# A drop mask added in PSUM in place of a masked exp, and P·V in column halves, in a top-32 attention kernel

## The chip, the cores and the metric

The kernel runs on one core of a Trainium2 chip. The core has five engines that run side by side: TensorE (PE, matrix products into PSUM; its weight loads are listed apart as PEld), VectorE (DVE), ScalarE (ACT), GpSimd (POOL) and SyncE (SP, which issues DMAs). The metric is the device time of one launch in microseconds; lower is better.

## The reference

Three stages follow one another. Only the first is touched by the change.

```python
# attention: q, k, v of shape (4, 8, 576, 64)
scores = scale * np.matmul(q, k.transpose(0, 1, 3, 2))
kth = np.partition(scores, -32, axis=-1)[..., -32:-31]     # the 32nd largest of each row
scores = np.where(scores >= kth, scores, -1e9)
attn = np.exp(scores - scores.max(-1, keepdims=True))
attn = attn / (attn.sum(-1, keepdims=True) + 1e-9)
x = np.matmul(attn, v)                                     # heads joined: (2304, 512)
# routing: each token to one of 8 experts, 288 tokens each; then the expert's relu FFN
# last: h = x @ w_in;  out = (h * cos(h)) @ w_out
```

So of each row of 576 scores only those not below the 32nd largest keep their exp, and the rest must weigh nothing in the product with V.

## The kernel before

**Tiles and groups.** The attention is cut into 144 tiles of 128 queries by 576 keys: for each of 16 pairs of heads four tiles of the one head, four of the other, and a ninth tile in which each head has its last 64 queries. Four tiles make a group, 36 groups in all.

**A step.** `run` (L429) goes through 42 steps. In one step seven groups are worked on, each at another stage, and four rounds u = 0 to 3 take one tile of each group:

- group A (newest): scores, two products of 288 keys into the PSUM tile `sp` (`qk_mm`, L185), copied by ACT to `S` (`qk_ev`, L189);
- group B: the eight largest of each of eight chunks of 72 keys on DVE (`chunks`, L195), and from them a lower bound of the threshold (`thresh`);
- group C: ACT forms a sign against that bound with its row sum (L226) and the exp `E` (L228); POOL multiplies sign and scores to `W` (`below`, L232);
- group D: DVE takes the eight largest of `W` (L244) and picks the exact 32nd score by rank (L241, `oh`; the table of ranks `R8` lies in the PSUM tile `av`); then `probs` (L253 to L269) makes the masked exp `P`. `PATTERN = "adap"` says how, by the tile's place in the group: `a`, a Sign on ACT (L266) and a product on POOL (L269); `d`, one instruction on DVE that compares and multiplies (L262); `p`, a comparison (L268) and a product (L269), both on POOL. The last eight tiles are `d`;
- group E: PE transposes `P` in blocks of 128 keys by a product with the identity (`tr` L277, `tr_tail` L283, 4.5 blocks for each tile), and ACT takes them out of PSUM with a Relu (L287, L293);
- group F: PE multiplies the turned P with V (`av`, L308 and L309), five products for each tile of 65 columns (64 of V and a column of ones for the sum). For a full tile all 128 queries are one product; the ninth tile of a pair has five products for the 64 queries of the one head, then five for the other;
- group G: DVE divides by the sum (`fin`, L315 to L338).

An fp32 product stands in the trace as two passes, each a weight load and a matmul; a transpose is one. Where a pair of heads is finished, its part of the routing logits is added: four transposes and a copy in one step (`logits_t`), five small products in the next (`logits_m`, L385).

**What sets the order.** Each engine's queue is the program's order, written out in `run`: the order of the calls within a round is the order on every engine, and semaphores tie the engines together. PSUM has eight banks: `sp` takes two twice, `pt` one twice, `av` and `ptail` one each.

The slow attention (`run_slow`) is for inputs that a check at the end flags, and does not run here.

## Time and profile before

| | us |
|---|---|
| median of three runs | 1247.97 |
| lowest, highest | 1246.42, 1253.18 |
| the profiled execution | 1246.51 |
| its span, first to last instruction | 1244.7 |
| steps in their steady state (scores of group 5 to group 36) | 43.4 to 429.7 |
| busy in the whole span: PE, DVE, ACT, POOL | 1131.7, 1058.9, 787.8, 603.3 |

The span is the sum of stages with different limits, so shares of the whole span say little. Attention fills roughly the first 480 us; what follows it is mostly PE. In the views below a step is seen best between two instructions that come once in each step, and idle time by what ended it. A matmul's duration in the trace runs past the start of the next one, since matmuls are pipelined: what a matmul costs is read from the distance between starts.

### The profile page before, as it was taken

The numbers are of one execution on the slowest core, as the hardware profiler recorded it, in microseconds if no ns is written. First come the engines' busy times: TensorE is split into PE (matmuls) and PEld (weight loads), VectorE is DVE, ScalarE is ACT, GpSimd is POOL, SyncE is SP. The second block draws the span as 40 slices with busy tenths as digits, with TensorE's granted clock in tenths as the row PEclk, the third lists the DMA queues.
The fourth block names the chain that finished last, engine by engine and source line by source line (L and its number), as shares of the span: only waits on it lengthen the run. The fifth ranks groups of instructions, "written<-read, shape, count | busy, mean of one in ns | idle before, by whom it ended". The sixth has DMA issues, their size and how long they took to land.

```text
span 1244.7 us, 22829 instructions
## 1 busy us (share of the span) xinstructions
PE 1131.7 (91%) x7449; PEld 996.6 (80%) x7449; DVE 1058.9 (85%) x4172; ACT 787.8 (63%) x1539; POOL 603.3 (48%) x592
## 2 busy tenths in 40 slices
PE   6799999999999986688898989989889999999996
PEld 4588787787878776578888889978777998999985
DVE  7999999999999984687888878699999668777774
ACT  6999989989998951333445446655655545444442
POOL 5999989989998960211000020164665343121120
PEclk9999999989998986698999989999898999999998
DMA  5111121121111001455555567522321100000000
GB/s 124 38 45 38 38 70 32 32 70 32 32 32 39 2 1 39 155 171 164 189 175 167 172 197 240 178 68 85 130 93 67 35 26 18 26 26 27 26 26 29
DMA packets 61890, 98.07 MB, mean 79 GB/s; under 512 B 30912, under 2 KB 30912, under 8 KB 61248
## 3 DMA queue, kind: packets, MB, share of 16 engines
q1 hardware_dynamic: 53648, 74.47, 19.6%
q10 hardware_dynamic: 5136, 12.60, 3.0%
q0 software_dynamic: 2976, 9.44, 2.3%
q8 instruction: 61, 1.00, 0.3%
q14 instruction: 69, 0.57, 0.1%
HBM read 78.66 MB, written 17.83 MB: 78 GB/s over the span
## 4 chain that ended last, share of the span: by engine, by line
PE 36%; DVE 32%; ACT 13%; issue 9%; POOL 5%; DMA 4%; POOLq 0%; DVEq 0%; SPq 0%; ACTq 0%
PE pa L1326 10%; PE y L1374 10%; DVE C L195 5%; PE pa L1174 4%; PE y L1189 4%; ACT sg L226 4%; DMA row<-x,i 3%; DVE w L244 3%; ACT E L228 3%; ACT S L189 2%; DVE wu L1256 2%; PE sp L185 2%; ACT PT L287 2%; PE av L308 2%; DVE ct L1334 2%
## 5 line engine op out<-in xcount | busy, mean ns | idle before, releaser
L1326 PE MATMUL pa<-yh,wu 128*128 128x384 f32 x1152 | 222.3, 340 | 10.7 <-POOL yh L1310 4.8
L1374 PE MATMUL y<-wu,gh 128*128 128x512 f32 x864 | 222.7, 402 | 5.6 <-POOL gh L1362 4.9
L1326 PEld LDWEIGHTS pa<-yh,wu 128*128 128x128 f32 x1152 | 206.0, 189 | 22.4 <-POOL yh L1310 6.4
L232 POOL TENSOR_TENSOR W<-sg,S 128x576 f32<-128x576 bf16 x144 | 197.8, 1379 | 33.0 <-ACT sg L226 31.6
L1374 PEld LDWEIGHTS y<-wu,gh 128*128 128x128 f32 x864 | 164.2, 192 | 38.9 <-POOL gh L1362 6.5
L185 PE MATMUL sp<-kT,qz 128*128 128x288 f32 x512 | 175.7, 433 | 12.7 <-ACT S L189 7.4
L195 DVE MAX8 C<-S 128x8 f32<-128x72 f32 x1152 | 162.5, 215 | 6.5 <-ACT S L189 6.3
L308 PE MATMUL av<-vm,PT 128*128 128x65 f32 (+1 forms) x1216 | 150.5, 274 | 13.7 <-DVE xb L331 7.5
L308 PEld LDWEIGHTS av<-vm,PT 128*128 128x128 f32 (+1 forms) x1216 | 139.1, 190 | 20.4 <-DVE xb L331 11.4
L1358 ACT ACTIVATE gh<-cx 128x384 fp32r<-128x384 f32 x95 | 49.9, 525 | 143.4 <-DVE cx L1356 140.9
L1151 POOL DMA_INDIRECT row<-x,i x24 | 29.5, 1231 | 215.9 <-DVE hh L1181 34.4
L269 POOL TENSOR_TENSOR P<-sg,E 128x576 f32<-128x576 bf16 x102 | 131.4, 1288 | 3.8
L1174 PE MATMUL pa<-xh,wu 128*128 128x288 f32 x768 | 124.9, 314 | 0.0
L277 PEld LDWEIGHTS pt<-ident,P 128*128 128x128 f32 x576 | 80.2, 145 | 52.7 <-POOL P L269 11.5
L1189 PE MATMUL y<-hh,wu 128*128 128x288 f32 x768 | 120.1, 306 | 0.0
L277 PE MATMUL pt<-ident,P 128*128 128x128 f32 x576 | 110.7, 279 | 6.0 <-POOL P L269 4.6
L1174 PEld LDWEIGHTS pa<-xh,wu 128*128 128x128 f32 x768 | 112.1, 201 | 3.2 <-issue 2.9
L226 ACT ACTIVATE sg<-S,tb 128x576 bf16<-128x576 f32 x144 | 111.7, 775 | 1.2
L228 ACT ACTIVATE E<-S,nmx 128x576 f32<-128x576 f32 x144 | 110.8, 769 | 0.0
L1189 PEld LDWEIGHTS y<-hh,wu 128*128 128x128 f32 x768 | 109.2, 196 | 1.7 <-ACT hh L1180 0.8
L189 ACT ACTIVATE S<-sp 128x576 f32<-128x576 f32 x144 | 92.5, 642 | 27.8 <-PE sp L185 27.7
L244 DVE MAX8 w<-W 128x8 f32<-128x576 f32 x144 | 104.6, 746 | 1.3 <-POOL W L232 1.2
(243 smaller groups left out, 2149.8 us busy)
## 6 DMA issues: line engine op xcount, KB each, us to landing
raw<-in_moe_w_dram SPq DMA_DIRECT2D x63, 512.0 KB, 3.9
kT<-in_k_dram SPq DMA_DIRECT2D x16, 288.0 KB, 3.2
qz<-in_q_dram SPq DMA_DIRECT2D x32, 128.0 KB, 3.2
vm<-in_v_dram SPq DMA_DIRECT2D x32, 128.0 KB, 3.0
x<-xb SPq DMA_DIRECT2D x4, 1024.0 KB, 4.1
r<-in_moe_w_in_dram ACTq DMA_DIRECT2D x8, 512.0 KB, 4.9
r<-in_moe_w_out_dram ACTq DMA_DIRECT2D x8, 512.0 KB, 5.0
half<-in_moe_w_in_dram SPq DMA_DIRECT2D x8, 512.0 KB, 3.7
```

The costliest lines, as they stand in the source:

```text
L185: s.nc.tensor.matmul(s.SP[j][:, c, :288], lh, s.KT[p][:, o + c * 288:o + c * 288 + 288], start=True, stop=True)
L195: s.nc.vector.max(c[:, e, :], s.SS[j][:, 72 * e:72 * e + 72])
L226: A.activation(s.SG[j], s.SS[j], AF.Sign, bias=s.TB[g][:, u:u + 1], scale=-EPS1, accum_out=s.SUM[g][:, u:u + 1])
L228: A.activation(s.EX[j], s.SS[j], AF.Exp, bias=s.NMX[g][:, u:u + 1])
L232: s.nc.gpsimd.tensor_tensor(s.W[j], s.SG.pop(j), s.SS[j], op=OP.mult)
L244: V.max(w8[:, u, :], s.W.pop(4 * g + u))
L277: s.nc.tensor.transpose(s.PT[j][:, i * 128:(i + 1) * 128], s.PB[j // 2][:, o + i * 128:o + (i + 1) * 128], s.k.ident)
L308: PEe.matmul(o[lo:hi, u, :], s.PT[j][:, c * 128 + lo:c * 128 + hi], t[:, a, c, :], start=c == 0, stop=False)
L1174: PEe.matmul(p, w[:, a, f * 128:(f + 1) * 128], XH[e, c][:, b, :], start=n == 0, stop=n == 11)
L1189: PEe.matmul(Y[e][m], w[:, a, o + m * 128:o + (m + 1) * 128], t[:, b, :], start=f == 0 and i == 0, stop=f == 7 and i == 2)
L1326: s.nc.tensor.matmul(p, w[:, a, f * 128:(f + 1) * 128], s.YH[q, c][:, b, :], start=n == 0, stop=n == 11)
L1374: PEe.matmul(O[q][m], g[:, a, m * 128:(m + 1) * 128], w[:, b, c:c + 512], start=first and j == 0, stop=last and j == 2)
```

## The change

Five edits, all in the attention:

1. The exp goes straight into `P`, unmasked; `E` is gone.
2. `probs` becomes `drops`: it writes no product, only a bf16 tile `mk` that is zero where the score stays and positive where it is dropped. Pattern "papp": `p`, POOL compares (is_lt); `a`, ACT takes a Relu of 2^64 times (threshold minus score); `d`, DVE compares, for the last eight tiles alone.
3. `turn` replaces each transpose by two products into the same block of PSUM: the transpose of `P`, and on top of it the product of `mk` with -4 times the identity, `minus`, in bf16. What is dropped becomes negative there, and the Relu that takes the block out of PSUM makes it zero.
4. `av` makes every product in two halves of 64 queries, in turn: chunk 0 for the first half, chunk 0 for the second, chunk 1 for the first, and so on.
5. The rank table `R8` moves from the bank of `av` to that of `ptail`, and both are now placed differently: `ptail` is one fixed bank, `av` a tile of the pool with one buffer.

```diff
--- before.py
+++ after.py
@@ -21,6 +21,7 @@
 
 EPS1 = 1.0 - 2.0 ** -24
 BIG = 2e37
+STEEP = 2.0 ** 64
 NB = 64
 NS, NR = 24, 4
 MAGIC = 1.5 * 2.0 ** 23
@@ -113,16 +114,18 @@
 class Attention:
 
 
-    PATTERN = "adap"
+    PATTERN = "papp"
 
     def __init__(s, k, sb, ps, slow=False):
         s.k, s.nc, s.sb, s.ps, s.slow = k, k.nc, sb, ps, slow
         s.tiles = head_tiles()
-        s.nsp, s.ntail = (1, 2) if slow else (2, 1)
+        s.nsp = 1 if slow else 2
         G = s.nc.gpsimd
-
-        s.B2 = ps.tile([128, 512], F32, name="av")
-        s.R8 = s.B2[:, 260:268]
+        s.minus = sb.tile([128, 128], BF, name="minus")
+        s.nc.vector.tensor_scalar(s.minus, k.ident, -4.0, None, op0=OP.mult)
+
+        s.B1 = ps.tile([128, 512], F32, name="ptail")
+        s.R8 = s.B1[:, 256:264]
         s.nc.vector.tensor_copy(s.R8, k.rank8)
 
         s.XB, s.XT = {0: s.x_tile()}, {0: s.x_tile(0)}
@@ -145,7 +148,7 @@
             s.QZ.append(z)
         s.QT, s.KT, s.SP, s.SS, s.CC, s.TB, s.NMX, s.SUM, s.M3 = ({} for _ in range(9))
         s.todo, s.turned = [], []
-        s.SG, s.EX, s.W, s.TB2, s.PB, s.PT, s.PTL, s.PTS, s.AVP = ({} for _ in range(9))
+        s.SG, s.MK, s.W, s.TB2, s.PB, s.PT, s.PTL, s.PTS, s.AVP = ({} for _ in range(9))
 
     def x_tile(s, tail=None):
         if tail is None:
@@ -224,8 +227,9 @@
             A.activation(s.TB[g], s.M3.pop(g)[:, :, 7], AF.Copy, scale=EPS1)
         s.SG[j] = sb.tile([128, S], BF, name="sg", bufs=5)
         A.activation(s.SG[j], s.SS[j], AF.Sign, bias=s.TB[g][:, u:u + 1], scale=-EPS1, accum_out=s.SUM[g][:, u:u + 1])
-        s.EX[j] = sb.tile([128, S], F32, name="E", bufs=10)
-        A.activation(s.EX[j], s.SS[j], AF.Exp, bias=s.NMX[g][:, u:u + 1])
+        if j % 2 == 0:
+            s.PB[j // 2] = sb.tile([128, 2 * S], F32, name="P", bufs=8)
+        A.activation(s.PB[j // 2][:, S * (j % 2):S * (j % 2) + S], s.SS[j], AF.Exp, bias=s.NMX[g][:, u:u + 1])
 
     def below(s, j):
         s.W[j] = s.sb.tile([128, S], F32, name="W", bufs=6)
@@ -248,39 +252,42 @@
         pick(3)
         yield
         s.TB2[g] = sb.tile([128, 4], F32, name="tb2", bufs=2)
-        s.nc.gpsimd.tensor_scalar(s.TB2[g], T, -EPS1, None, op0=OP.mult)
-
-    def probs(s, j, kind):
+        s.nc.gpsimd.tensor_scalar(s.TB2[g], T, STEEP, None, op0=OP.mult)
+
+    def drops(s, j, kind):
 
         nc, sb = s.nc, s.sb
         g, u = divmod(j, 4)
         T = s.k.tall[:, 1, j:j + 1]
-        if j // 2 not in s.PB:
-            s.PB[j // 2] = sb.tile([128, 2 * S], F32, name="P", bufs=5)
-        P = s.PB[j // 2][:, S * (j % 2):S * (j % 2) + S]
-        if kind == "d":
-            nc.vector.scalar_tensor_tensor(P, s.SS[j], T, s.EX[j], op0=OP.is_ge, op1=OP.mult)
-            return
-        m = sb.tile([128, S], BF, name="sg2", bufs=4)
+        if j // 2 not in s.MK:
+            s.MK[j // 2] = sb.tile([128, 2 * S], BF, name="mk", bufs=5)
+        m = s.MK[j // 2][:, S * (j % 2):S * (j % 2) + S]
         if kind == "a":
-            nc.scalar.activation(m, s.SS[j], AF.Sign, bias=s.TB2[g][:, u:u + 1], scale=EPS1)
+
+            nc.scalar.activation(m, s.SS[j], AF.Relu, bias=s.TB2[g][:, u:u + 1], scale=-STEEP)
         else:
-            (nc.vector if kind == "m" else nc.gpsimd).tensor_scalar(m, s.SS[j], T, None, op0=OP.is_ge)
-        nc.gpsimd.tensor_tensor(P, m, s.EX[j], op=OP.mult)
-
+            (nc.vector if kind == "d" else nc.gpsimd).tensor_scalar(m, s.SS[j], T, None, op0=OP.is_lt)
+
+
+    def turn(s, out, d, o):
+
+        PEe, m = s.nc.tensor, s.MK.get(d)
+        PEe.matmul(out, s.PB[d][:, o:o + 128], s.k.ident, is_transpose=True, start=True, stop=m is None)
+        if m is not None:
+            PEe.matmul(out, m[:, o:o + 128], s.minus, start=False, stop=True)
 
     def tr(s, j, half):
         if half == 0:
             s.PT[j] = s.ps.tile([128, 512], F32, name="pt", bufs=2)
         o = 640 * (j % 2)
         for i in (0, 1) if half == 0 else (2, 3):
-            s.nc.tensor.transpose(s.PT[j][:, i * 128:(i + 1) * 128], s.PB[j // 2][:, o + i * 128:o + (i + 1) * 128], s.k.ident)
+            s.turn(s.PT[j][:, i * 128:(i + 1) * 128], j // 2, o + i * 128)
 
     def tr_tail(s, j):
         g, u = divmod(j, 4)
         if u == 1:
-            s.PTL[g] = s.ps.tile([128, 2, 128], F32, name="ptail", bufs=s.ntail)
-        s.nc.tensor.transpose(s.PTL[g][:, u // 2, :], s.PB[j // 2][:, 512:640], s.k.ident)
+            s.PTL[g] = s.B1[:, :256].rearrange("p (a b) -> p a b", a=2)
+        s.turn(s.PTL[g][:, u // 2, :], j // 2, 512)
 
     def tr_ev(s, j):
         t = s.sb.tile([128, 512], F32, name="PT", bufs=4 if s.slow else 9)
@@ -301,11 +308,14 @@
             if two and g % 2 == 0:
                 s.AVP[g] = s.ps.tile([128, 2, 512], F32, name="sp", bufs=s.nsp)[:, 0, :260].rearrange("p (a b) -> p a b", a=4)
             else:
-                s.AVP[g] = s.B2[:, :260].rearrange("p (a b) -> p a b", a=4)
+                s.AVP[g] = s.ps.tile([128, 4, 65], F32, name="av")
         o = s.AVP[g]
-        for a, lo, hi in (((hs, 0, 128),) if hs < 2 else ((0, 0, 64), (1, 64, 128))):
-            for c in range(4):
+
+        halves = tuple((hs if hs < 2 else z, 64 * z, 64 * z + 64) for z in range(2))
+        for c in range(4):
+            for a, lo, hi in halves:
                 PEe.matmul(o[lo:hi, u, :], s.PT[j][:, c * 128 + lo:c * 128 + hi], t[:, a, c, :], start=c == 0, stop=False)
+        for a, lo, hi in halves:
             PEe.matmul(o[lo:hi, u, :], s.PTS[g][:, u // 2, lo:hi], tt[:, j % 2, a, :], start=False, stop=True)
 
     def fin(s, g, ends):
@@ -491,10 +501,10 @@
                 if ok(gD) and u >= 1:
                     for w in ((0, 1), (2,), (3,))[u - 1]:
                         kind = pat(4 * gD + w)
-                        if kind not in "dm":
-                            s.probs(4 * gD + w, kind)
-                if ok(gD) and pat(4 * gD + u) in "dm":
-                    s.probs(4 * gD + u, pat(4 * gD + u))
+                        if kind != "d":
+                            s.drops(4 * gD + w, kind)
+                if ok(gD) and pat(4 * gD + u) == "d":
+                    s.drops(4 * gD + u, "d")
                 if ok(gB):
                     s.chunks(4 * gB + u)
                 if u == 0 and step in when:
@@ -565,7 +575,7 @@
     V = k.nc.vector
     n = k.tall.shape[2]
     bad = big(0, 3 * n, F32)
-    V.tensor_scalar(bad[:, :n], k.tall[:, 1], 1e-25, None, op0=OP.is_lt)
+    V.tensor_scalar(bad[:, :n], k.tall[:, 1], 1e-11, None, op0=OP.is_lt)
     yield
     mant = big(1, 2 * n, I32)
     V.tensor_scalar(mant.rearrange("p (a b) -> p a b", a=2), k.tall.bitcast(I32), 0x7FFFFF, None, op0=OP.bitwise_and)
```

The names in the rows below: `sp` scores, `pt` and `ptail` the turned blocks, `P` exp, `mk` and `minus` the mask and its factor, `vm`, `vt` V, `PT`, `PTt` the turned P in SBUF, `sg` a sign or comparison, `W` the product for the threshold, `tb` the threshold's bias.

On PE, from the last scores of a round with a tail block to the first two tiles of the products with V. Before:

```order
L185 MATMUL sp<-kT,qz_183 128x288
L277 MATMUL pt<-ident,P 128x128 x2
L283 MATMUL ptail<-ident,P 128x128
L308 MATMUL av<-vm_129,PT 128x65 x4
L309 MATMUL av<-vt_135,PTt 128x65
L308 MATMUL av<-vm_129,PT 128x65 x4
L309 MATMUL av<-vt_135,PTt 128x65
```

Now:

```order
L188 MATMUL sp<-kT,qz_171 128x288
L275 MATMUL pt<-ident,P 128x128
L277 LDWEIGHTS mk
L277 MATMUL pt<-minus,mk 128x128
L275 MATMUL pt<-ident,P 128x128
L277 LDWEIGHTS mk
L277 MATMUL pt<-minus,mk 128x128
L275 MATMUL ptail<-ident,P 128x128
L277 LDWEIGHTS mk
L277 MATMUL ptail<-minus,mk 128x128
L317 MATMUL av<-vm_132,PT 64x65 x8
L319 MATMUL av<-vt_138,PTt 64x65 x2
```

Every transposed block has a mask product behind it, and the products of one tile are ten instructions of 64 queries in place of five of 128.

On POOL, one step, with the engines whose semaphore an instruction waits for. Before:

```order
L251 TENSOR_SCALAR tb_3013<-tall 128x4 [waits DVE_49]
L232 TENSOR_TENSOR W<-sg,S 128x576 [waits Activation_49] x2
L269 TENSOR_TENSOR P<-sg_3077,E 128x576 [waits PE_49,Activation_49]
L232 TENSOR_TENSOR W<-sg,S 128x576 [waits Activation_49]
L269 TENSOR_TENSOR P<-sg_3124,E 128x576 [waits PE_49,Activation_49]
L232 TENSOR_TENSOR W<-sg,S 128x576 [waits Activation_49]
L268 TENSOR_SCALAR sg_3165<-S,tall 128x576
L269 TENSOR_TENSOR P<-sg_3165,E 128x576 [waits Pool_49]
```

Now:

```order
L255 TENSOR_SCALAR tb_3555<-tall 128x4 [waits DVE_49]
L236 TENSOR_TENSOR W<-sg,S 128x576 [waits Activation_49,Pool_49]
L236 TENSOR_TENSOR W<-sg,S 128x576 [waits Activation_49]
L269 TENSOR_SCALAR mk<-S,tall 128x576 [waits PE_49]
L236 TENSOR_TENSOR W<-sg,S 128x576 [waits Activation_49,Pool_49]
L269 TENSOR_SCALAR mk<-S,tall 128x576 [waits PE_49]
L236 TENSOR_TENSOR W<-sg,S 128x576 [waits Activation_49,Pool_49]
L269 TENSOR_SCALAR mk<-S,tall 128x576
```

Three products and one comparison of a step have become three comparisons.

On PE, the first tail block of a step with its neighbours and their waits. Before:

```order
L277 MATMUL pt<-ident,P 128x128 [waits DVE_49]
L277 MATMUL pt<-ident,P 128x128
L185 MATMUL sp<-kT,qz_177 128x288
L277 MATMUL pt<-ident,P 128x128 x2
L283 MATMUL ptail<-ident,P 128x128 [waits Activation_49]
L185 MATMUL sp<-kT,qm_178 128x288 [waits DMAHW4_49,DMAHW3_49,Activation_49]
```

Now:

```order
L275 MATMUL pt<-ident,P 128x128
L277 LDWEIGHTS mk
L277 MATMUL pt<-minus,mk 128x128
L275 MATMUL ptail<-ident,P 128x128 [waits DVE_49,Activation_49]
L277 LDWEIGHTS mk
L277 MATMUL ptail<-minus,mk 128x128
L188 MATMUL sp<-kT,qz_171 128x288 [waits DMAHW6_49,DMAHW5_49,Activation_49]
```

The first tail block of a step now waits for DVE, whose picks read the rank table in the same bank.

## Rows read from the trace of the kernel before

**Rows 1.** Stretches: us; busy PE, PEld, DVE, ACT, POOL (count); PE clock; DMA share, GB/s
```profile
297.60:309.20 11.60, 11.48 (x90) 9.66 (x89) 11.57 (x79) 11.57 (x26) 11.48 (x11) 1.00 0.01 2
...
370.70:386.50 15.80, 15.07 (x96) 12.81 (x95) 14.50 (x90) 11.86 (x26) 13.77 (x14) 0.78 0.01 2
...
sum 112.70, PE 107.87 PEld 91.26 DVE 110.44 ACT 106.87 POOL 102.16; mean PE 11.99 PEld 10.14 DVE 12.27 ACT 11.87 POOL 11.35
...
43.40:429.70 386.30, 368.68 (x2601) 311.97 (x2600) 378.46 (x2453) 366.84 (x758) 352.70 (x311) 0.96 0.14 38
```

**Rows 2.** Timeline, ACT: start, duration, engine, line
```profile
390.57 0.76 ACT L266 ACTIVATE sg<-S,tb 128x576 bf16<-128x576 f32 x1
...
391.24 0.63 ACT L189 ACTIVATE S<-sp 128x576 f32<-128x576 f32 x1
```

**Rows 3.** By source line: durations in ns, least/median/most
```profile
L262 DVE SCALAR_TENSOR_TENSOR P<-S,tall,E x42: 797/964/1891, 28.1 to 466.6; 128x576 f32<-128x576 f32 x42
...
L232 POOL TENSOR_TENSOR W<-sg,S x144: 1271/1290/1936, 18.8 to 452.9; 128x576 f32<-128x576 bf16 x144
...
L268 POOL TENSOR_SCALAR sg<-S,tall x34: 1717/1726/1740, 35.4 to 444.3; 128x576 bf16<-128x576 f32 x34
...
L269 POOL TENSOR_TENSOR P<-sg,E x102: 1276/1288/1299, 30.4 to 446.1; 128x576 f32<-128x576 bf16 x102
```

**Rows 4.** Timeline, PE: products with V, scores, transposes
```profile
180.92 1.06 PE L308 MATMUL av<-vm,PT 128*128 128x65 f32 x8
...
182.03 0.70 PE L185 MATMUL sp<-kT,qz 128*128 128x288 f32 x2
182.57 0.38 PE L277 MATMUL pt<-ident,P 128*128 128x128 f32 x2
182.79 0.65 PE L185 MATMUL sp<-kT,qz 128*128 128x288 f32 x2
...
183.50 0.65 PE L185 MATMUL sp<-kT,qz 128*128 128x288 f32 x2
```

**Rows 5.** Timeline, PE and its weight loads, around a ninth tile
```profile
186.21 0.38 PE L277 MATMUL pt<-ident,P 128*128 128x128 f32 x2
...
186.52 0.60 PEld L308 LDWEIGHTS av<-vm,PT 128*64 128x64 f32 x10 [0.17 <-issue]
...
187.04 0.14 PEld L308 LDWEIGHTS av<-vm,PT 128*64 128x64 f32 x1
187.04 0.14 PEld L309 LDWEIGHTS av<-vt,PTt 128*64 128x64 f32 x1
187.10 0.37 PEld L308 LDWEIGHTS av<-vm,PT 128*64 128x64 f32 x5
...
187.65 0.30 PEld L308 LDWEIGHTS av<-vm,PT 128*128 128x128 f32 x2
```

**Rows 6.** Transposes' weight loads: count, busy us, mean ns, idle before them
```profile
L277 PEld LDWEIGHTS pt<-ident,P 128*128 128x128 f32 x532 | 74.8, 144 | 52.5 <-POOL P L269 11.5 <-issue 4.5
```

**Rows 7.** Timeline, PE, bf16 products in the routing
```profile
746.22 0.39 PE L915 MATMUL pa<-yh,yh 128*128 128x36 bf16 x9
```

**Rows 8.** Timeline of one step around its first tail block
```profile
258.35 0.27 PE L283 MATMUL ptail<-ident,P 128*128 128x128 f32 x1
...
258.93 0.21 DVE L241 SCALAR_TENSOR_TENSOR oh<-av,sum,w 128x8 f32<-128x8 f32 x1
...
259.16 0.65 PE L185 MATMUL sp<-kT,qz 128*128 128x288 f32 x2
...
262.75 0.63 ACT L189 ACTIVATE S<-sp 128x576 f32<-128x576 f32 x1
```

**Rows 9.** Timeline, end of the attention, POOL and DVE
```profile
448.16 6.57 POOL L232 TENSOR_TENSOR W<-sg,S 128x576 f32<-128x576 bf16 x4
...
449.05 6.30 DVE L262 SCALAR_TENSOR_TENSOR P<-S,tall,E 128x576 f32<-128x576 f32 x4
```

## The prediction

> **What bounds the kernel now.** I read first the busy time by stretch, since attention is the only stage touched: the 31 steps from 43.4 to 429.7 take 386.3 us, and nine of them that hold one turn of the pattern take 112.70 [rows 1]. What the reader is to see there is that no engine stands out. In the step from 297.60 PE shows 11.48, DVE 11.57, ACT 11.57 and POOL 11.48 of 11.60. The PE figure says little, because the recorded ends of matmuls overlap the next ones; so I went to the timeline for the distance between starts. The ACT figure is the hard one: ACT works through its queue without a gap, and over the nine steps it is busy 106.87 of 112.70. Of its 5.83 us of idle time 3.94 lie in the one step from 370.70, where the granted clock is 0.78 on average, that is, half of it was at the lower level (1.2 GHz) after PE had waited. So outside that step ACT is idle 1.9 us in eight steps. DVE (110.44) seems just as full, but part of that is stretched time: its compare-and-multiply lasts from 797 to 1891 ns for one and the same shape, and POOL's product `W` from 1271 to 1936 [rows 3]; each waits for the other when they meet.
>
> **ACT, the term that sets the end.** A step has four scores, four exps, four signs, four copies of the turned P and two `a` tiles; it will have one `a` tile. From the start of the `a` Sign to the start of the next ACT instruction it is 0.67 us [rows 2], and the Relu that stays in its place has the same shapes. Nine steps lose 9 x 0.67 = 6.0 us: 106.87 becomes 100.8.
>
> **DVE.** The compare-and-multiply leaves the steady steps: at least 0.80, in the mean nearer 1.2 [rows 3]. The plain step's 11.57, which holds one at its least, becomes 10.8. DVE was level with ACT and stays just below it.
>
> **POOL.** Before: four `W` at 1.29, three products at 1.29 and one comparison at 1.73, 10.8 by the medians, more where `W` is stretched. Now: four `W` at 1.29 and three comparisons at 1.73, 10.4 [rows 3], and what stretched `W` is gone. So POOL gets 0.4 to 0.9 per step back and is not the end either.
>
> **PE, the term that could eat all of it.** Without the logits a step is, by starts [rows 4]: one tile's scores and transposes 2 x 0.71 = 1.42; a tail block 0.11 for every second tile; one tile's products with V 1.11. Four tiles: 5.68 + 0.22 + 4.44 = 10.3 us. Two things happen to it.
>
> The halves. Before the change the ninth tile of each pair already ran in halves, though one after the other, and its rows show what two halves do when they meet: at 187.04 the last loads of the first half and the loads of the second start together, and the next come 0.06 later [rows 5]. The five loads from 187.10 last 0.37 for a load of 0.14, so 0.058 from one to the next in one half. Two halves in turn should therefore go at two passes in 0.058: ten such slots, 0.58 us, for a tile's twenty passes. Going into and out of half width costs something: the transposes before it (0.11 apart) would have let the first load start at 186.43, and it came at 186.52; from there to the next full-width load at 187.65 are 1.13 us for 20 passes, of which three pairs met, so 17 slots, 0.99. In and out together 0.23. The step has two batches of two tiles: 2 x (1.16 + 0.23) = 2.78 against 4.44, a gain of 1.66.
>
> This is where the Trainium skill speaks against the change. "TensorE: Matmul & The Clock Gate", part 3 on packing small matmuls, says that a weight load overlaps matmuls in flight only where their row groups differ; two column halves share all rows. By that rule there would be no gain at all. The rows at 187.04 contradict it on this chip, and I go by them; the rule's outcome is the second rival below.
>
> The masks. Eighteen products in bf16 are added to a step, each a load of 128 columns and 128 moving columns; no row has exactly that. Nine bf16 products of 36 columns follow one another in 0.39 us with the last one's tail, so loading bf16 weights hides in about 0.025 [rows 7]; the mask's load will hide behind the transpose in front. Its own matmul then delays the next instruction by the larger of its stream and that one's load. A full-width fp32 load keeps the next product 0.11 away however few columns that has: the passes with V, of 65 columns, come ten in 1.11 [rows 4]. That is the upper end, 18 x 0.11 = 2.0. A transpose's load is recorded at 144 ns [rows 6], about as a half-width load at 0.14 [rows 5], which came every 0.058: where a transpose follows, about 0.055, and if it were so everywhere 18 x 0.055 = 1.0 would be the lower end. By the order half of the masks in `pt` stand before a transpose and half before scores, so I take the middle, 0.08: 1.4 us. I exclude a gain below zero, since nothing is taken away for a mask.
>
> Together PE goes from 10.3 to about 10.05, with bounds of 9.6 and 10.6 (10.3 - 1.66 + 1.0 and + 2.0). PE gets no faster to speak of; it merely stays under ACT's 10.9 for a plain step (11.57 - 0.67).
>
> **The new wait.** The first tail block of a step now waits for DVE's last pick of that step, because the rank table lies in its bank. In the step shown the tail block started at 258.35 and the last pick came after 258.93 and ended near 259.15 [rows 8], so PE would have stood 0.8 us. Behind it queue the scores of round 2. Those started at 259.16 and ACT read them at 262.75, more than 2 us after they were done [rows 8], so the wait is covered by ACT's lag; without that cover it would cost up to 0.8 in each step. The old wait, `av` for DVE's pick, goes with the bank. The masks' loads wait for POOL or ACT as the transposes did for `P`, a step ahead, and nothing is queued behind them that did not wait before.
>
> **The ends.** In the two steps before 43.4 ACT, DVE and POOL are the limits already: two times 0.67, 1.3 us. At the end, four `W` on POOL took 6.57 and four compare-and-multiply on DVE 6.30, side by side [rows 9], where four `W` alone are 5.2: the comparisons that stay read one large operand in place of two and should let POOL finish 1.4 earlier, and DVE by at least that. A shorter product with V and longer transposes cancel there. I take 1.9 for the end.
>
> **The sum.** Nine steps: 100.8 of ACT, 2.5 of idle time (1.9 now, a little more since four engines come still nearer to each other), and half of the 3.9 that the low clock costs: 1.9. I halve it because PE's waits ahead of it become shorter, but where they fall in the new cadence no row tells. That is 105.2 against 112.70, 7.5 less; 386.3 / 112.7 = 3.43 turns give 25.7. With 1.3 and 1.9 it is 28.9 off the profiled execution's 1246.5 (its span 1244.7 and 1.8 around it): 1217.6. The median of the runs shown lies 1.5 above that execution, so 1219.
>
> **Rivals.**
> - *The clock.* Either all low stretches in the steady steps stay (half of 3.9 back on each turn: +6.6, 1226) or none does (1212). Both belong to the likeliest case, whose own range is 1209 to 1228. The low stretch in every nine steps speaks for their staying; that PE has more work in shorter steps, against.
> - *The halves run one after the other (slower than before).* Twenty passes at 0.058 and half of 0.23 are 1.28 per tile against 1.11, 0.66 per step; with the masks' 1.4 PE gains 2.1 and takes 12.4 for a plain step of 11.6 now: 0.8 x 31 = 25, so 1272. It decides as soon as a step needs more than 1.3 us extra on PE. For it: two passes of one half follow each other in the queue before the other half's come, and in the ninth tile the second half got going only when three passes were left of the first. Against it: in the new order the other half is at most two passes away.
> - *PE becomes the floor.* Masks at 0.11 (+0.3 net) and the tail block's wait of 0.8 uncovered give 11.4 for a plain step: 0.2 x 31 = 6 less, 1241. For it: PE's margin under ACT is only 0.3 to 0.9. Against it: if PE is late, DVE's pick is no longer behind it, so the two prices hardly fall together.
> - *POOL holds up ACT's work.* If comparisons on POOL stretched as `W` did, by 0.4 each, a step would be 11.6 again: no gain. Their 34 rows lie between 1717 and 1740 [rows 3], so I give this nothing of its own.
>
> **Chances and range.** Likeliest 0.73 (1219), PE the floor 0.15 (1241), halves serial 0.12 (1272). The range reaches up to the middle of the floor case, 1242, and down to 1205, where all low stretches go and the masks cost their least. About 0.5%, 6 us, is what can be told from no change. Faster by more: 0.73 and half of the floor case, 0.81; within it: 0.07; slower: 0.12.
>
> **What would show it.** In the steady steps the busy time by stretch should show steps near 10.9 to 11.5, ACT without gaps and POOL's `W` at 1.29 throughout; loads of the two halves starting together, 0.06 apart, a tile in 0.58; 0.055 from a mask to a transpose and 0.11 from a mask to scores. I am wrong if ACT waits for scores in most steps (PE is the floor), or if a tile's products take over 1.1 us.

## The result and the profile after

The changed kernel takes 1210.22 us (median of four runs, 1208.27 to 1213.56) against 1250.58 for the kernel before (four runs, 1246.42 to 1253.49): a ratio of 0.968 [0.964, 0.972]. The prediction was 1219, in a range of 1205 to 1242. Its profiled execution took 1213.56 us with a span of 1211.6, so 33.1 less span than before.

A step is measured here from the start of ACT's first copy of scores in one group to that in the next. The steady stretch, cut as before, runs from the last copy of the fifth group to that of the thirty-sixth, 31 steps. Between the two profiled executions the time went as follows:

| stretch | before | after | difference | forecast |
|---|---|---|---|---|
| up to the fifth group's last scores | 43.4 | 41.5 | −1.9 | −1.3 |
| 31 steady steps | 386.3 | 359.8 | −26.5 | −25.7 |
| then to the first product of the experts | 84.4 | 79.6 | −4.7 | −1.9 |
| from there to the end | 730.6 | 730.7 | +0.1 | 0 |

| a step, median us | plain | with the logits' transposes and copy | with the logits' small products |
|---|---|---|---|
| before | 11.61 | 12.13 | 12.61 |
| after | 10.95 | 11.63 | 11.85 |

The busy time by stretch answers to [rows 1] (us; busy PE, PEld, DVE, ACT, POOL with counts; granted clock; DMA share, GB/s): a plain step, one with the logits' transposes, one with their small products, and all 31 steps.

```profile
172.00:182.90 10.90, 10.53 (x135) 8.47 (x134) 10.84 (x78) 10.87 (x24) 9.64 (x9) 1.00 0.01 2
359.70:371.30 11.60, 11.23 (x139) 8.94 (x138) 11.49 (x82) 11.55 (x25) 10.32 (x10) 1.00 0.27 104
371.30:383.20 11.90, 11.73 (x145) 9.61 (x143) 10.84 (x79) 11.20 (x25) 10.82 (x10) 1.00 0.01 3
41.50:401.30 359.80, 347.96 (x4250) 280.20 (x4250) 345.08 (x2414) 349.08 (x726) 327.23 (x280) 1.00 0.15 41
```

In the plain step ACT is busy 10.87 of 10.90: it is full, and the step is as long as ACT's work. DVE stands right under it, at 10.84. In the second row both are nearly full, DVE at 11.49 and ACT at 11.55 of 11.60. In the third row ACT is not: 11.20 of 11.90. Over all 31 steps ACT has 10.7 us of idle time. The clock of the whole stretch is 1.00 where it was 0.96: the four stretches at 1.2 GHz that lay in the steady steps before (at 63.7, 152.5, 265.1 and 377.8) have no successor. Three of them made steps of 15.75 to 15.88 us, where the other nine of that kind took 12.27 in the mean, and the first made a plain step of 13.25 in place of 11.61; so by estimate about 12 us of the 26.5 are the clock's.

By source line the answer to [rows 3] (durations in ns, least, median and most; first and last start):

```profile
L236 POOL TENSOR_TENSOR W<-sg,S x144: 1276/1292/1505, 17.7 to 423.5; 128x576 f32<-128x576 bf16 x144
...
L269 POOL TENSOR_SCALAR mk<-S,tall x102: 1716/1727/1742, 29.0 to 416.2; 128x576 bf16<-128x576 f32 x102
L269 DVE TENSOR_SCALAR mk<-S,tall x8: 510/624/1545, 420.2 to 435.1; 128x576 bf16<-128x576 f32 x8
```

`W`, which reached 1936 ns before, takes 1292 in the median and at most 1505, in the drain; POOL's comparisons are not stretched by anything.

The two halves of the products with V, by their weight loads (start, duration; in brackets the idle time ahead). It is the view of [rows 5], in a batch of two tiles:

```profile
355.68 0.55 PEld L317 LDWEIGHTS av<-vm,PT 128*64 128x64 f32 x16 [0.16 <-issue]
356.14 0.20 PEld L319 LDWEIGHTS av<-vt,PTt 128*64 128x64 f32 x4
356.25 0.55 PEld L317 LDWEIGHTS av<-vm,PT 128*64 128x64 f32 x16
356.72 0.20 PEld L319 LDWEIGHTS av<-vt,PTt 128*64 128x64 f32 x4
356.99 0.30 PEld L188 LDWEIGHTS sp<-kT,qz 128*128 128x128 f32 x2
```

From one tile's first load to the next tile's it is 356.25 − 355.68 = 0.57 us, for twenty passes. A full-width tile took 1.11 [rows 4].

The masks on PE (timeline, start and duration), between the scores of two tiles:

```profile
358.46 0.27 PE L275 MATMUL pt<-ident,P 128*128 128x128 f32 x1
358.57 0.22 PE L277 MATMUL pt<-minus,mk 128*128 128x128 bf16 x1
358.62 0.28 PE L275 MATMUL pt<-ident,P 128*128 128x128 f32 x1
358.74 0.22 PE L277 MATMUL pt<-minus,mk 128*128 128x128 bf16 x1
358.80 0.70 PE L188 MATMUL sp<-kT,qz 128*128 128x288 f32 x2
359.34 0.27 PE L275 MATMUL pt<-ident,P 128*128 128x128 f32 x1
```

From transposes to transposes it is now 359.34 − 358.46 = 0.88 us, where scores and two transposes took 0.71 [rows 4]: two masks cost 0.17.

One thing is new in the list of waits of the steady stretch (waiting instruction, what came last, us in total, times, longest):

```profile
...
PEld ptail L275 <- ACT sg L229: 18.0, 31, 1.3
PE ptail L275 <- DVE rinv L327: 10.7, 30, 0.7
DVE L L400 <- PE pt L395: 8.9, 9, 1.0
...
ACT S L192 <- PE sp L188: 8.7, 20, 0.6
...
DVE oh L245 <- ACT PTt L300: 0.6, 1, 0.6
```

PE's load for `ptail`, the first tail block, stands once in each of 31 steps, up to 1.3 us. The arrows give the engines, ACT and DVE, but the lines named (a sign, a reciprocal) neither read nor write `ptail`. Which instruction holds the load back is read from the timeline of one such step:

```profile
346.40 0.40 ACT L300 ACTIVATE PTt<-ptail 128x256 f32<-128x256 f32 x1
...
346.84 0.23 DVE L245 SCALAR_TENSOR_TENSOR oh<-ptail,sum,w 128x8 f32<-128x8 f32 x1
...
348.67 0.22 DVE L245 SCALAR_TENSOR_TENSOR oh<-ptail,sum,w 128x8 f32<-128x8 f32 x1
348.81 0.08 DVE L245 DVE_READ_ACCUMULATOR oh<-ptail,sum,w 128x1 f32 x1
349.01 0.14 PEld L275 LDWEIGHTS ptail<-ident,P 128*128 128x128 f32 x1 [0.37 <-ACT sg L229]
...
352.63 0.64 ACT L192 ACTIVATE S<-sp 128x576 f32<-128x576 f32 x1
...
353.72 0.25 DVE L400 TENSOR_TENSOR L<-L,pt 128x32 f32<-128x32 f32 x2 [0.97 <-PE pt L395]
...
358.66 0.65 ACT L192 ACTIVATE S<-sp 128x576 f32<-128x576 f32 x1 [0.56 <-PE sp L188]
```

ACT copies the tail blocks out until 346.80, DVE's four picks of the same bank begin at 346.84, the last ends at 348.89, and the load of PE's first tail block starts 0.12 later. Of the last three rows the first is ACT's copy of the scores of round 2, which did not have to wait. The other two came late: DVE stands 0.97 for PE's small products before it adds them to the logits (`L`), and ACT 0.56 for the first scores of the next group. In the kernel before, the tail block of the step shown ran 0.58 ahead of a pick [rows 8].

### The profile page after: what moved, and what is told of

Its sections match the earlier page's. It is cut to its first block, busy times and chain, and to the rows that moved or that the text cites. A ratio compares the mean times of both kernels' runs of the same rounds, so it can differ in the third digit from the quotient of the medians.

```text
span 1211.6 us, 26491 instructions
## 1 busy us (share of the span) xinstructions
PE 1109.5 (92%) x9377; PEld 962.3 (79%) x9377; DVE 1020.0 (84%) x4139; ACT 768.4 (63%) x1505; POOL 574.9 (47%) x558
## 4 chain that ended last, share of the span: by engine, by line
PE 44%; DVE 34%; ACT 10%; issue 6%; DMA 4%; POOL 2%; SPq 0%; DVEq 0%; POOLq 0%; ACTq 0%
PE pa L1336 11%; PE y L1384 11%; PE pa L1184 5%; PE y L1199 5%; DVE C L198 4%; DVE w L248 4%; PE sp L188 3%; DMA row<-x,i 3%; DVE wu L1266 3%; ACT sg L229 3%; PE av L317 2%; ACT P L232 2%; ACT S L192 2%; PE pt L395 2%; ACT PT L294 2%
## 5 line engine op out<-in xcount | busy, mean ns | idle before, releaser
L236 POOL TENSOR_TENSOR W<-sg,S 128x576 f32<-128x576 bf16 x144 | 186.5, 1296 | 31.1 <-ACT sg L229 31.0
L188 PE MATMUL sp<-kT,qz 128*128 128x288 f32 x512 | 179.4, 440 | 6.0 <-ACT S L192 4.7
L269 POOL TENSOR_SCALAR mk<-S,tall 128x576 bf16<-128x576 f32 x102 | 176.2, 1728 | 0.0
L198 DVE MAX8 C<-S 128x8 f32<-128x72 f32 x1152 | 159.5, 218 | 5.5 <-ACT S L192 5.2
L275 PE MATMUL pt<-ident,P 128*128 128x128 f32 x576 | 129.6, 281 | 0.0
L277 PE MATMUL pt<-minus,mk 128*128 128x128 bf16 x576 | 113.9, 222 | 0.4 <-POOL mk L269 0.4
L232 ACT ACTIVATE P<-S,nmx 128x576 f32<-128x576 f32 x144 | 110.7, 769 | 0.0
L248 DVE MAX8 w<-W 128x8 f32<-128x576 f32 x144 | 104.9, 749 | 0.1
L1343 DVE TENSOR_SCALAR ct<-pa 128x384 f32<-128x384 f32 x95 | 52.7, 555 | 57.0 <-PE pa L1336 56.6
```

What stands on the lines that cost most here:

```text
L188: s.nc.tensor.matmul(s.SP[j][:, c, :288], lh, s.KT[p][:, o + c * 288:o + c * 288 + 288], start=True, stop=True)
L198: s.nc.vector.max(c[:, e, :], s.SS[j][:, 72 * e:72 * e + 72])
L232: A.activation(s.PB[j // 2][:, S * (j % 2):S * (j % 2) + S], s.SS[j], AF.Exp, bias=s.NMX[g][:, u:u + 1])
L236: s.nc.gpsimd.tensor_tensor(s.W[j], s.SG.pop(j), s.SS[j], op=OP.mult)
L248: V.max(w8[:, u, :], s.W.pop(4 * g + u))
L269: (nc.vector if kind == "d" else nc.gpsimd).tensor_scalar(m, s.SS[j], T, None, op0=OP.is_lt)
```

## The experiments

Five questions stood open: whether ACT sets the steps, whether the halves alone or the masks alone explain the gain, what the order of the halves is worth, what the new wait costs, and why the clock stays up. "Steady" below is the stretch of 31 steps in the profiled execution.

**1. The halves alone.** The kernel before, with the products with V in alternating halves and nothing else.

```diff
-        for a, lo, hi in (((hs, 0, 128),) if hs < 2 else ((0, 0, 64), (1, 64, 128))):
-            for c in range(4):
+        halves = tuple((hs if hs < 2 else z, 64 * z, 64 * z + 64) for z in range(2))
+        for c in range(4):
+            for a, lo, hi in halves:
                 PEe.matmul(o[lo:hi, u, :], ...)
+        for a, lo, hi in halves:
             PEe.matmul(o[lo:hi, u, :], ...)
```

> The kernel before, with nothing but the products with V in alternating halves. Theory A (ACT sets the pace of the steady steps, PE only in those with the small logits products): plain steps stay at 11.6 and those with the logits copy at 12.1, those with the small products fall from 12.5 toward 12.0; 1238 to 1252 us, depending on the low-clock stretches, which PE's extra idle time may well make more of. Theory B (PE was the limit before, and the halves are the gain): 1.66 less in each step, about 1195 to 1205.

Measured: 1228.29 us (1227.65 to 1231.03), less than the range expected, ratio 0.986 [0.976, 0.995]; steady 376.1, steps of 11.62, 12.15 and 11.63. Plain steps and those with the transposes did not move by 0.02: PE was not their floor. The steps with the small products fell from 12.61 (12.45 without the three at the low clock) to 11.63, more than expected: in these alone PE was the floor. The waits (41 to 395 us) say the same, since PE's loads now stand idle for ACT's copies of scores:

```profile
PEld sp L185 <- ACT S L189: 22.0, 25, 1.8
```

Of the 18.9 us of span that this profile has less than the kernel before, only 10.2 lie in the steady steps; 5.3 lie between them and the experts and 2.8 behind, where profiles of one kernel differ by more than that.

**2. The masks alone.** The changed kernel with the full-width products of before.

```diff
-        halves = tuple((hs if hs < 2 else z, 64 * z, 64 * z + 64) for z in range(2))
-        for c in range(4):
-            for a, lo, hi in halves:
+        for a, lo, hi in (((hs, 0, 128),) if hs < 2 else ((0, 0, 64), (1, 64, 128))):
+            for c in range(4):
                 PEe.matmul(o[lo:hi, u, :], ...)
-        for a, lo, hi in halves:
             PEe.matmul(o[lo:hi, u, :], ...)
```

> The changed kernel with the products with V full width as before, masks kept. Theory A (the halves pay for the masks): PE needs 1.66 more a step, 11.9 in plain steps and near 13 in those with the small logits products, so it becomes the limit: about 1240 to 1250 us, the gain gone. Theory B (the masks hide in PE's idle time, the halves are not needed): 1208 to 1216.

Measured: 1250.73 us (ten runs, 1240.88 to 1253.99), ratio 1.001 [0.997, 1.005]; steady 396.5, steps of 11.99, 12.62 and 13.19. ACT has 0.67 less per step in it and nothing comes of it, because PE with 18 masks and full-width products needs 12.0: the steady steps are 10.2 longer than before. The rank table lies with `ptail` here too, but the tail block's loads waited in one place only (2.5 us), so it is not the table's place that eats the gain. Neither half of the change gains without the other what both gain together.

**3. The halves apart.** As changed, but all products of the one half ahead of those of the other.

```diff
-        halves = tuple((hs if hs < 2 else z, 64 * z, 64 * z + 64) for z in range(2))
-        for c in range(4):
-            for a, lo, hi in halves:
+        for a, lo, hi in tuple((hs if hs < 2 else z, 64 * z, 64 * z + 64) for z in range(2)):
+            for c in range(4):
                 PEe.matmul(o[lo:hi, u, :], ...)
-        for a, lo, hi in halves:
             PEe.matmul(o[lo:hi, u, :], ...)
```

> The changed kernel with all five products of one half first, then the five of the other. Theory A (only neighbours in the queue run together, about three passes of them, as in the ninth tile before): a batch of two tiles takes 31 slots of 0.058 in place of 20, 1.3 us more a step, 1230 to 1240 us. Theory B (the array takes the two halves together in whatever order): a tile stays at 0.58 and the time at 1208 to 1214.

Measured: 1237.26 us (ten runs, 1231.43 to 1240.3), ratio 0.991 [0.987, 0.996]; steady 383.2, steps of 11.54, 12.33 and 12.74. The timeline of PE shows one batch of two tiles, up to the next full-width instruction:

```profile
208.33 0.74 PE L316 MATMUL av<-vm,PT 128*64 128x65 f32 x10
208.85 0.22 PE L317 MATMUL av<-vt,PTt 128*64 128x65 f32 x1
208.91 0.22 PE L316 MATMUL av<-vm,PT 128*64 128x65 f32 x1
208.91 0.22 PE L317 MATMUL av<-vt,PTt 128*64 128x65 f32 x1
...
210.28 1.27 PE L393 MATMUL pt<-wg,xT 128*128 128x8 f32 x10
```

The batch takes 210.28 − 208.33 = 1.95 us, where in alternation it takes 356.99 − 355.68 = 1.31. The halves meet only at their ends (both start at 208.91). The difference, 0.64 a batch and 1.28 a step, makes PE the floor; a plain step loses 0.6. So the gain of halves is that of two in flight, and the order in the queue decides it.

**4. No masks.** As changed, with the transposes alone in `turn`.

```diff
-        PEe, m = s.nc.tensor, s.MK.get(d)
+        PEe, m = s.nc.tensor, None
```

> The changed kernel without the mask products on PE (so no score is dropped); the masks are still made on POOL and ACT. Theory A (PE with the masks is the limit only in steps with the small logits products): these fall from 11.8 to about 11.1, plain steps stay at 10.95: 1198 to 1204 us if the clock stays up. Theory C (the masks' work is what kept the clock up): low stretches come back in the steady steps, about 3.9 us each for three of them, and the time is 1208 to 1216.

Measured: the whole time, 6481 us, says nothing, since a second attention and another routing follow. The steady steps can be read: 355.0 in all, 10.94 for a plain one, 11.48 with the transposes and 11.57 in the median (11.06 to 12.03) with the small products. One short stretch in the first of them, at 47.5, is at 1.2 GHz, and none behind it. The theory that the masks' work keeps the clock up falls. So does the theory that the masks set the steps with the small products: these fell by 0.28 only and stay uneven. PE has less to do here and comes earlier to the tail block, and stands there longer (41 to 396 us; in the changed kernel 10.7, 30 times):

```profile
PE ptail L275 <- DVE rinv L327: 36.2, 25, 2.1
```

**5. The rank table back in the bank of `av`.** This undoes the fifth edit alone.

```diff
-        s.B1 = ps.tile([128, 512], F32, name="ptail")
-        s.R8 = s.B1[:, 256:264]
+        s.B2 = ps.tile([128, 512], F32, name="av")
+        s.R8 = s.B2[:, 260:268]
...
-            s.PTL[g] = s.B1[:, :256].rearrange("p (a b) -> p a b", a=2)
+            s.PTL[g] = s.ps.tile([128, 2, 128], F32, name="ptail")
...
-                s.AVP[g] = s.ps.tile([128, 4, 65], F32, name="av")
+                s.AVP[g] = s.B2[:, :260].rearrange("p (a b) -> p a b", a=4)
```

> The changed kernel with the rank table back in the bank of av (ptail a pool tile again), so that the first tail block of a step no longer waits for DVE's pick and the products with V do. Theory A (in the steps with the small logits products the pick, PE's work behind the tail block, and DVE's add of the logits form one loop, which sets 11.84 there): these steps fall to about 11.5, PE's own work; plain steps stay at 10.95; about 5 us less, 1203 to 1207. Theory B (PE's work alone sets those steps): no change, 1208 to 1214.

Measured: **1199.36 us** (1194.98 to 1203.49), ratio to the kernel before 0.960 [0.953, 0.967]; steady 350.1, which is 9.7 less than in the changed kernel and more than theory A expected, with steps of 10.94, 11.46 and 11.32: those with the transposes fell too. The wait for `ptail` is gone from the list (of the steady stretch), ACT's waits for scores are down from 8.7 to 3.0, and DVE's for the small products from 8.9 to 1.8:

```profile
...
ACT S L192 <- PE sp L188: 3.0, 12, 0.3
...
DVE L L400 <- PE pt L395: 1.8, 5, 0.4
```

By stretch, a step with the transposes, one with the small products, and all 31:

```profile
282.55:294.02 11.47, 10.86 (x137) 8.63 (x135) 11.41 (x80) 11.44 (x25) 11.05 (x11) 1.00 0.23 63
294.02:305.36 11.34, 11.34 (x144) 9.40 (x142) 11.08 (x80) 11.08 (x25) 10.36 (x10) 1.00 0.10 24
41.40:391.50 350.10, 346.01 (x4267) 280.00 (x4269) 344.46 (x2420) 346.12 (x726) 326.77 (x281) 1.00 0.15 43
```

Now ACT is full in the step with the transposes too (11.44 of 11.47), with DVE right under it. In the step with the small products ACT and DVE have 0.26 to spare and PE has no gap: the chain of work that ended last runs through that step on PE alone. The tail block no longer waits for the picks; in the timeline of one step it starts between the second and the third:

```profile
293.98 0.21 DVE L245 SCALAR_TENSOR_TENSOR oh<-av,sum,w 128x8 f32<-128x8 f32 x1
...
294.69 0.14 PEld L275 LDWEIGHTS ptail<-ident,P 128*128 128x128 f32 x1
...
294.79 0.21 DVE L245 SCALAR_TENSOR_TENSOR oh<-av,sum,w 128x8 f32<-128x8 f32 x1
```

This version beats both kernels in its steps; against the changed kernel the intervals of the whole ratio just overlap, so the 9.7 us of the steps are the firmer number.

**6. A second Relu on ACT.** As changed, with one more tile of a group masked by ACT and one fewer by POOL.

```diff
-    PATTERN = "papp"
+    PATTERN = "aapp"
```

> The changed kernel with pattern aapp: a second Relu on ACT in each step in place of a comparison on POOL. Theory A (ACT sets plain and copy steps): plain steps 10.95 + 0.67 = 11.6, copy steps 11.63 + 0.5 to 0.67, steps with the small products 11.84 to 12.0; about 12 to 18 us more, 1222 to 1228. Theory B (POOL sets them): plain steps get shorter, below 1208.

Measured: 1226.92 us (1223.12 to 1227.66), ratio 0.980 [0.973, 0.987]; steady 371.6, steps of 11.60, 12.13 and 11.99. One Relu more costs a plain step 0.65, one Sign less had given 0.66, and POOL has a comparison less in it: ACT sets plain steps in the changed kernel. With two `a` tiles ACT's work makes a step of 11.60 here, as long as a plain step of the kernel before; there DVE was as full as ACT [rows 1], so that one of the two alone set its steps was not shown.

**7. DVE's addition of the logits later.** In the changed kernel DVE waits for the small products (`L` in the waits above) ahead of its picks. Here the addition stands one round later, to see whether that is what delays the picks.

```diff
-        pl = pl[:, :5 * E].rearrange("p (a e) -> p a e", e=E)
+        s.sums.append((pl[:, :5 * E].rearrange("p (a e) -> p a e", e=E), b, hp, q))
+
+    def logits_a(s):
...
                 if u == 3:
+                    s.logits_a()
                     s.logits_t()
```

> The changed kernel with DVE's add of the logits one round later, behind the last eight chunk maxima, so that DVE does not stand about 1 us for PE's small products. Theory A (the loop through pick, tail block, small products and add sets those steps): from 11.84 to about 11.5, where PE's own work ends it: 1203 to 1207. Theory B (PE's work alone): no change.

Measured: 1203.18 us (1200.62 to 1206.62), ratio 0.963 [0.956, 0.970], the number of theory A, but not by its mechanism: the steady stretch is 360.1, as in the changed kernel, and what was gained lies behind it. There the stretch from the first product of the experts to the end, which no kernel of this study touches, took between 723 and 734 us from profile to profile, 723 in this one and 731 in the changed kernel's. Within the steady stretch the steps moved: 10.94 for a plain one, 11.47 in the median with the transposes (11.63 before this edit) and 11.99 with the small products (11.85). One of each kind together takes 23.46, as against 23.48. DVE now stands for ACT's copy out of `ptail` ahead of its picks, which it did once, for 0.6 us, in the changed kernel (41 to 395 us):

```profile
DVE oh L245 <- ACT PTt L300: 12.4, 22, 1.4
```

So the addition was one link, and a second path of nearly the same length stood behind it. In the changed kernel the chain of work that ended last shows the first one (start, duration):

```profile
348.76 0.14 DVE oh L245 x2
...
349.05 0.30 PE ptail L275
...
352.48 1.21 PE pt L395 x10
...
353.72 0.25 DVE L L400 x2
...
358.90 0.21 DVE oh L245 x2
```

It goes from DVE's picks to PE's first tail block, along PE's queue to the small products, over the addition to DVE, and stays on DVE to the picks of the next step and through that step. With the addition out of the way it goes along PE's queue to the next scores, then through ACT to its copy of the tail blocks and to DVE's picks. Both begin with the tail block that waits for the picks, and that is what the table's place makes.

**8. Both: table back and addition later.**

> Both: rank table back with av, and the add a round later. Theory A: as good as the better of the two, not the sum, since PE's own work of about 11.5 is the next floor in those steps: 1202 to 1206. Theory B: 1208 to 1214.

Measured: 1206.95 us (1202.9 to 1209.52), ratio 0.964 [0.957, 0.971]; steady 355.2, with a stretch at 1.2 GHz at 303.2 and steps of 10.95, 11.47 and 11.55. It is no better than the table back alone; why the later addition costs something there was not followed.

**9. Every mask product twice.** The same product is added once more, so that a dropped score becomes more negative still.

```diff
+            PEe.matmul(out, m[:, o:o + 128], s.minus, start=False, stop=False)
             PEe.matmul(out, m[:, o:o + 128], s.minus, start=False, stop=True)
```

> The changed kernel with every mask product made twice (the result is the same after the Relu). The second one stands behind a bf16 product with bf16 weights, so by the price of a stream of 128 columns it should cost 0.055 each, 18 in a step: PE 1.0 more. If that is the price: PE passes ACT in all steps, plain about 11.2, copy and small-product steps about 12.0 to 12.8; 1230 to 1240 us. If a mask costs a full 0.11: plain 12.2, 1255 or more. If masks hide in PE's idle time: no change.

Measured: 1225.18 us (1221.37 to 1229.42), ratio 0.985 [0.977, 0.992]; steady 374.7, steps of 11.28, 12.07 and 12.48. Eighteen products more lengthen a plain step by 0.33 only, since PE first uses up its margin under ACT. On PE itself the second product costs 0.055 (timeline):

```profile
200.03 0.22 PE L277 MATMUL pt<-minus,mk 128*128 128x128 bf16 x1
200.09 0.22 PE L278 MATMUL pt<-minus,mk 128*128 128x128 bf16 x1
200.14 0.28 PE L275 MATMUL pt<-ident,P 128*128 128x128 f32 x1
```

18 x 0.055 = 1.0 on PE and 0.33 on the step leave 0.66: by this estimate that was PE's margin in a plain step. The whole time lies below the range expected.

**10. The rank table in SBUF.** The picks read it from there and share no bank with anything.

```diff
-        s.R8 = s.B1[:, 256:264]
-        s.nc.vector.tensor_copy(s.R8, k.rank8)
+        s.R8 = k.rank8
```

> The changed kernel with the rank table read from SBUF, in no bank of PSUM. If the wait of the tail block is all that the table's place costs: as the table with av, 1196 to 1203 us, copy steps 11.3 and small-product steps 11.5. Rival: with both inputs in SBUF DVE's pick meets POOL's work and each of the four picks of a step stands up to a POOL instruction (1.3 to 1.7): picks of 1 us and more, 1210 to 1235 us.

Measured: 1204.34 us (1199.18 to 1205.67), ratio 0.967 [0.960, 0.974]; steady 354.7. The plain steps, those with the transposes (11.46) and four with the small products (11.31) are those of the table back in `av`; the other eight take 11.82 to 11.98. It lies between: the shared bank is gone, but a pick with two operands in SBUF, 205 ns in the median, took up to 1080 (by source line: least, median, most). In the eight longer steps the first pick takes 557 to 681 ns, in three of the four shorter ones 199 to 207 and in the fourth 473; but plain steps have such picks too and are no longer for it, so that they are the cause is not shown:

```profile
L244 DVE SCALAR_TENSOR_TENSOR oh<-rank,sum,w x144: 197/205/1080, 25.5 to 425.5; 128x8 f32<-128x8 f32 x144
```

**11 and 12. Both kernels once more,** for the clock: one more profile each, nothing changed.

> The kernel before, unchanged, for a second profile. If its low-clock stretches belong to the program: again four in the steady steps, one each 112 us. If they come and go from run to run: other places or another number, with the same step lengths between them (11.6, 12.15, 12.5).

> The changed kernel, unchanged, for a second profile. If the clock staying up in the steady steps belongs to the program: again no low stretch between 50 and 400 us, and steps of 10.95, 11.63 and 11.84; if it was luck: some.

Measured: before 1250.57 us, steady 382.4, five stretches at 1.2 GHz behind 52 us (63.9, 152.6, 238.0, 289.2, 374.5; the first two where they were, the others not); after 1213.59 us, steady 361.6, none behind 52 us, but one of 3.4 us at 47.9, which makes the first whole steady step 12.88 long in place of 10.95. The medians of each kind of step agree between the two profiles of a kernel to 0.06. So behind 52 us the low stretches came in both profiles of the one program and in neither of the other; at the start of the steady steps they came in both programs (43.3 and 43.4 in the kernel before). More than that two profiles of each do not show.

## Why the prediction was right, and where it was not

*ACT sets the end, and loses 0.67 per step.* Right for plain steps. One was forecast at 10.9 and is 10.95, with ACT busy 10.87 of 10.90; one Relu more puts the 0.65 back (experiment 6). DVE's 10.8 is 10.84, just below ACT as forecast. What sets the steps with the logits' work is told under the wait below.

*The halves.* Right. A tile in 0.58 was forecast and 0.57 measured; a batch with its switches 1.39 and 1.31. "TensorE: Matmul & The Clock Gate" in the Trainium skill, part 3, lets a weight load overlap matmuls in flight only where their row groups differ. The trace does not agree with that sentence: two column halves of all rows do overlap (twenty passes in 0.57 us, where ten of full width take 1.11), and how much they do hangs on the order of the queue (0.64 a batch, experiment 3). The rival in which the halves run one after the other is excluded for this order; even with the halves apart the result was not slower than before.

*The masks.* Right: 0.17 for a pair, of which 0.055 stand ahead of a transpose (358.57 to 358.62 as against 358.46 to 358.57 for the transpose's own 0.11) and 0.11 ahead of scores by difference. That they cost as much as the halves save was the point of the sum on PE, and experiments 1 and 2 show it from either side: without the halves the masks eat the whole gain.

*POOL.* Right. In the median its comparisons take 1.727 and its `W` 1.292, and only the drain stretches `W`, to 1.505.

*"The wait is covered by ACT's lag."* This is the step that failed: the wait was put at nothing, and it cost 9.7 us. It was argued from a single step of the kernel before, in which the scores of round 2 were read 3.6 us after PE started their second half. Plain steps paid nothing indeed (10.95 with the wait and 10.94 without it); there PE has 0.66 to spare (experiment 9). In the step of the changed kernel shown above, too, ACT reads the scores of round 2 (352.63) 2.0 us after PE has gone on to the transposes behind them (350.66). What the argument left out is the rest of PE's queue behind the tail block: the small products, for which DVE stood 0.97, and the next group's scores, for which ACT stood 0.56. DVE has no time to spare in the step that follows (11.49 of 11.60), so its picks come late again, and the tail block behind them. Steps with logits work came out at 11.63 and 11.85, above the 10.9 to 11.5 that were to be seen; the table back in the other bank gives 11.46 and 11.32 and takes 9.7 us off the 31 steps (experiment 5). The Trainium skill, "PSUM — Partial Sum Buffer", section "PSUM bank collisions raise a hardware error", tells authors to guard PSUM by bank and quadrant and not by address. The trace agrees that it was so guarded here: `R8` and the blocks share no address, and the tail block waits for the picks in all 31 steps.

*The low clock.* Mis-sized. Half of it was to remain, 1.9 for nine steps; none did in this profile, and in the second one 1.9 in all 31 steps. By the terms of the sum, for nine steps: 104.9 measured (359.8 / 3.43) against 105.2 forecast, and this near hit is luck, two errors that cancel, the clock 1.9 too dear and the tail block's wait 2.8 (9.7 / 3.43) too cheap, with idle time 1.3 in place of 2.5 once that wait is away (350.1 / 3.43 = 102.1, and 100.8 is ACT). Why the clock stays up is open, and with it the cause of about 12 of the 26.5 us. It is not the masks' work (experiment 4); the halves alone still leave three low stretches (86.2, 99.9 and 260.3), the masks with full-width products two short ones (178.7 and 243.5), and both with the halves apart none.

*The ends.* The start gave 1.9 for 1.3. The drain gave 4.7 for 1.9, but that is no firm figure: the second profiles have 98.0 and 76.3 for 84.4 and 79.6, and experiment 1, which keeps the masked exp, has 79.1. POOL's last group of `W` ends 25.0 us behind the steady steps in the kernel before and 23.7 in the changed one, the 1.4 that was forecast. Most of the 4.7 lies further on, between a product of the routing's range (L409, now L419) and the routing's first (L787, now L797), 17.9 before and 13.0 after, with a granted clock of 0.66 and 0.95:

```profile
470.90:488.80 17.90, 14.12 (x95) 12.84 (x95) 5.26 (x26) 2.66 (x5) 0.00 (x0) 0.66 0.18 67
441.90:454.90 13.00, 9.22 (x136) 7.82 (x133) 5.27 (x26) 2.71 (x6) 0.00 (x0) 0.95 0.25 92
```

One reason that was given did not hold: the comparisons on DVE are still stretched beside POOL's `W`, though they read one large operand now. The rows (timeline) answer to [rows 9]:

```profile
419.29 5.69 POOL L236 TENSOR_TENSOR W<-sg,S 128x576 f32<-128x576 bf16 x4
...
420.17 5.12 DVE L269 TENSOR_SCALAR mk<-S,tall 128x576 bf16<-128x576 f32 x4
```

The four `W` alone lost 0.9 of the 1.4, and the four comparisons take 1.28 each in the mean. What else shortened the end was not tried apart.

*The time.* Between the two profiled executions 33.1 us of span went, against 28.9 in the sum. The rest of the way from 1219 to 1210 is in the runs: the forecast was set 1.5 above its execution, and the median of the changed kernel lies 3.3 below the profiled one. Runs of the kernel before spread from 1237 to 1262 over the study, so single microseconds of a whole time decide nothing here; lengths of steps do.

## What to carry to other kernels

Where two changes trade one engine's time for another's, work out each engine's floor for both together: here the masks alone made the steady steps 10.2 us longer, the halves alone 10.2 shorter, and the two together 26.5, the low clock's part included. Before a small read-only table is put in a PSUM bank, list who writes and reads that bank in the loop, and follow everything that stands in the queue behind the instruction that will wait: its next reader may have slack, and a later one none. When products are cut into column halves, let the halves alternate in the queue.

## What the runs showed of the hardware that was not expected

- Column halves meet only if they stand next to each other in the queue: 1.31 us for a batch in alternation, 1.95 with the halves apart, about 2.2 at full width (experiment 2 has 201.52 to 203.75 for two tiles in its timeline).
- A bf16 product of 128 columns added to a block that an fp32 transpose has just written costs 0.055 us ahead of another bf16 product or a transpose, and 0.11 ahead of fp32 scores.
- A comparison on DVE with one large fp32 operand and a bf16 result takes 0.51 us at its least and up to 1.55 while POOL multiplies with two operands in SBUF.
- A pick of 8 elements from two SBUF operands on DVE, 0.205 us in the median, took up to 1.08; with one of them in PSUM the picks shown took 0.20 to 0.23.
- In both profiles of the kernel before PE ran at 1.2 GHz in four or five stretches between 52 us and the end of the steady steps, in both of the changed kernel in none; in the first profiles PE is busy in 95 and 97% of the steady steps.
